# A transformer block on one core: the second feed-forward product by 15 products over thirds instead of 7 over halves, the out projection in full, the blocks in one written order

## The chip, the cores and the metric

The kernel runs on one core of one Trainium2 chip. The engines of the core that matter here: TensorE (PE) multiplies matrices, VectorE (DVE), ScalarE (ACT) and GpSimd (POOL) work element by element, and SyncE (SP) issues DMA transfers. Each engine executes its own queue of instructions in the order in which they were written; between engines they wait for each other by semaphores. SBUF is the working memory of 128 partitions, PSUM the eight banks (0 to 7) into which TensorE accumulates.

The metric is the device time of one execution, in microseconds; the numbers are medians over repeated executions.

## The reference

One block of a transformer with adaptive layer norm over 2048 tokens of 576 channels. The attention is linear (32 heads of 18 channels, a feature map from a softmax of both signs), the feed-forward part goes to 4608 channels and back:

```python
S, D, H, Dff = 2048, 576, 32, 4608
sa, ca, ga, sb, cb, gb = (silu(c) @ w_mod) in six rows of D
h = layernorm(x) * (1 + ca) + sa
q, k, v = h @ wqkv, by heads
phi(a) = concat(softmax(a @ w_phi), softmax(-(a @ w_phi)))
kv, z = phi(k)^T v, sum over tokens of phi(k)
o = (phi(q) kv) / (phi(q) z + 1e-6)
x = x + ga * (o @ wo)
h = layernorm(x) * (1 + cb) + sb
x = x + gb * (relu(h @ w1) @ w2)
```

All inputs are bf16. The two feed-forward products carry most of the work: per token 2 x 576 x 4608 multiplications.

## The kernel before

**Tiles and blocks.** The tokens are 16 tiles of 128, taken two at a time: 8 blocks of 256 tokens, numbered 0 to 7. In the first part (to about 88 us) the kernel computes the modulation, all keys and values, and `kv`; queries, softmax and the first tiles' attention follow. Then come the blocks' feed-forward parts, each a first product (`h @ w1`, relu) and a second one (`@ w2`). While block b is in its feed-forward part, the tiles of block b+1 are normalized and turned, and the attention and the out projection of block b+2 are done in between.

**Order.** All work up to the end of block 0 is written out as a list of words in a string, `ORDER`; each word stands for a function in the table `JOBS`, and the words' order is the order in which instructions are issued to the engines' queues. Blocks 1 to 7 run in a loop: `l1_seven(b, hooks)` for the first product, by another string of words (`SEVEN`), then `l2(b, hooks)` for the second. Both call hooks at numbered places, `in_seven(b)` and `in_l2(b)`, and these put the other blocks' work in.

**First product.** In blocks 1 to 7 it is computed by the seven-product scheme of Strassen and Winograd over quarters: words such as `M1_0|M5_0` are pairs of matmuls on 64 partitions (line 793), the words `A`, `B`, `C`, `d` add intermediate results on ScalarE and VectorE, and `k11_g` to `k22_g` (line 823) take the relu of a group g of four row tiles into SBUF. Four differences of the activations' quarters (`t_feat`, line 851, four instructions on VectorE) are needed ahead of it; they read `h2`, the normalized and turned tiles.

**Second product.** The relu's result of a block is a matrix of 36 row tiles (4608 channels) by 256 tokens. It is cut in halves: 18 row tiles each, 128 tokens each, and `w2` by 18 row tiles and 288 columns. The seven-product scheme needs 7 products (`prod`, line 873) of 18 matmuls of 128 x 128 weights and 288 columns: A11 B11, A12 B21, U2 T2, A11' T1, U3 T3, A22 T4 and A12' B22. The sums of weights T1 to T4 (`t_part`, line 515, 12 instructions of 1728 columns on VectorE) are made once, in block 0; the sums of activations U2 and U3 are made in each block's first product (lines 819 and 820), and A11' = A11 + U2 and A12' = A12 - U2 in its second (lines 881 and 884, 2304 columns). The products share three PSUM banks, X = 2, Y = 4 and Z = 3: bank X collects partial sums, and ScalarE copies its state out after three of the products (`copy`, line 877, tile `RS`). `fin` (lines 853 to 862) then forms an output of 128 x 288 by an addition on VectorE (line 860, or a multiplication, line 858), a multiplication with `gb` on POOL (line 861) and an addition to `x_sb` on POOL (line 862); SyncE stores the tile.

**The last block's end.** The last of the 7 products is done in two parts of 144 columns (line 910) with `gb` already multiplied into the weights (`scale_b22`), so that a single VectorE addition (line 911) and the store (line 912) follow.

**Layer norm and h turn.** In the first product of block b, the tiles of block b+1 are added up (`add_res` or `seven_add`), their mean and variance taken (`bn`, `ln2_rs`), normalized on VectorE (`ln2_apply`, line 438, two instructions per tile, tile `xn`), and turned by a DMA that SyncE issues (line 416, `h2<-xn`; in this text the h turn). In the second product of block b, ScalarE scales the nine parts of `h2` (`h_scale`, line 1045), and then `t_feat` follows.

**Attention and out projection.** In the second product of block b the attention of block b+2's tiles is finished (`num_mm`, line 404; `num_o`, lines 411 and 412) and turned by SyncE (line 416, `oT<-o_sb`). For the tiles of blocks up to 3 the out projection is `project`: 16 matmuls of 288 columns (line 957) and four on 64 partitions (line 964). In blocks 2 to 5 (`B7 = 2`) it is `seven_wo` for the blocks two further on: by the seven-product scheme, 14 matmuls (line 982) and four on 64 partitions (line 987), with sums of activations by `seven_sums` on VectorE (lines 992 to 995), copies on ScalarE (lines 1002, 1015) and additions on POOL (lines 1003, 1017). Its weight sums are `wo_sum`.

The engine queue is therefore decided by the strings and the hook positions alone; no scheduler moves anything.

## Time and profile before

| | |
|---|---|
| runs | 373.72, 372.51, 373.53 us; median 373.53 |
| profiled execution: span from its first to its last instruction | 372.0 us |
| the page names no other time of the profiled execution; median of the runs less span | 1.53 us |
| TensorE busy | 364.3 us (98%) |
| VectorE busy | 292.7 us (79%) |
| ScalarE busy | 232.9 us (63%) |
| GpSimd busy | 131.0 us (35%) |
| granted TensorE clock | full in all 40 slices |
| length of blocks 3, 4 and 5, product by product (217.77, 252.39, 287.01, 321.62 us are starts of second products) | 34.62, 34.62, 34.61 us |

The page is one profiled execution. Its busy times are means over stages with different limits, so the prediction reads windows (the busy time of each engine in a stretch of the span), the chain of work that ended last (followed back from the last instruction), groups of instructions (a line, an engine, an operation, output and inputs, shape, count, then busy time, mean duration in ns, and the idle time ahead of them with what ended it), and a few rows of the timeline (start, length, engine, line, operation, count, in brackets the wait ahead of it). PE are matmuls, PEld the weight loads that run beside them; SPq is SyncE's queue.

### The profile page before, as it was taken

How to read it: one execution, taken by the hardware profiler on the slowest of the kernel's cores; microseconds unless marked ns; L12 is line 12 of the kernel's file. 1: busy time of each engine (PE TensorE's matmuls, PEld its weight loads, DVE VectorE, ACT ScalarE, POOL GpSimd, SP SyncE). 2: the span in 40 equal slices, each digit the busy share in tenths (PEclk: the TensorE clock that was granted, in tenths of full speed). 3: DMA queues.
4: the chain of work that ended last, by engine and by line, in shares of the span. 5: the costliest groups of instructions: out<-in, count | busy, mean ns of one | idle time of the engine just before them, and what ended most of it. 6: DMA issues, size and time to landing. Idle time of an engine off the chain costs nothing.

```text
span 372.0 us, 14787 instructions
## 1 busy us (share of the span) xinstructions
PE 364.3 (98%) x6486; PEld 312.1 (84%) x6486; DVE 292.7 (79%) x538; ACT 232.9 (63%) x499; POOL 131.0 (35%) x183
## 2 busy tenths in 40 slices
...
GB/s 290 361 336 389 275 395 246 323 226 279 224 226 168 86 57 109 82 129 85 52 85 128 35 51 115 99 35 73 95 67 19 86 19 51 35 2 36 4 2 33
DMA packets 58913, 50.28 MB, mean 135 GB/s; under 512 B 46944, under 2 KB 51168, under 8 KB 58080
## 3 DMA queue, kind: packets, MB, share of 16 engines
...
q10 hardware_dynamic: 144, 0.16, 0.1%
...
HBM read 32.27 MB, written 5.90 MB: 103 GB/s over the span
## 4 chain that ended last, share of the span: by engine, by line
PE 83%; DMA 7%; DVE 5%; SPq 2%; issue 1%; ACT 1%; DVEq 0%
PE PS L873 29%; PE PS L793 27%; PE PS L282 15%; PE PS L776 4%; DMA R<-in_wqT_dram 3%; PE PS L982 2%; DMA R<-in_wsc_dram 2%; DMA oT<-o_sb 2%; SPq L363 2%; PE PS L334 2%; PE PS L404 1%; DMA eqd<-RT 1%; PE PS L957 1%; DVE R L489 1%; DVE Rq L292 1%
## 5 line engine op out<-in xcount | busy, mean ns | idle before, releaser
L861 POOL TENSOR_TENSOR yt<-yt,gb_row 128x288 f32<-128x288 f32 x23 | 27.6, 1199 | 185.8 <-DVE yt L860 185.8
L793 PEld LDWEIGHTS <-R 64*128 64x128 bf16 (+1 forms) x2128 | 88.8, 94 | 0.8 <-issue 0.2
L873 PEld LDWEIGHTS <-RH 128*128 128x128 f16 x738 | 71.1, 98 | 18.2
L793 PE MATMUL PS<-h,R 64*128 64x128 bf16 x1232 | 80.9, 216 | 0.0
L823 ACT ACTIVATE RH<-PS 128x512 f16<-128x512 f32 x112 | 59.3, 603 | 10.8 <-PE PS L793 10.7
L873 PE MATMUL PS<-R,RH 128*128 128x288 bf16 (+1 forms) x486 | 65.0, 286 | 0.0
L793 PE MATMUL PS<-RE,R 64*128 64x128 f16 x896 | 56.2, 216 | 0.0
L287 ACT ACTIVATE RT<-PS,rs 128x576 bf16<-128x576 f32 x64 | 42.5, 748 | 10.3 <-PE PS L282 9.0
L793 PE MATMUL PS<-h,early 64*128 64x128 bf16 x448 | 37.5, 216 | 0.0
L1045 ACT ACTIVATE h<-h,mod 128x256 bf16<-128x256 bf16 x63 | 32.7, 588 | 2.2 <-DMA h<-xn 2.2
L873 PE MATMUL PS<-RT,RH 128*128 128x288 f16 x252 | 33.8, 286 | 0.0
L249 DVE BATCH_NORM_STATS2 st<-x_sb 128x6 f32<-128x288 bf16 x64 | 25.7, 443 | 7.9 <-DMA x_sb<-in_xk_dram 7.8
L282 PE MATMUL PS<-RH,RT 116*128 116x288 bf16 x240 | 31.9, 286 | 0.0
L282 PE MATMUL PS<-RH,R 116*128 116x288 bf16 x240 | 31.5, 286 | 0.3
L793 PEld LDWEIGHTS <-w 64*128 64x128 f16 (+1 forms) x560 | 30.8, 94 | 0.0
L793 PE MATMUL PS<-RE,w 64*128 64x128 f16 x448 | 30.1, 216 | 0.0
L793 PE MATMUL PS<-RE,x_sb 64*128 64x128 f16 x448 | 29.2, 216 | 0.0
L793 PEld LDWEIGHTS <-early 64*128 64x128 bf16 x448 | 28.2, 94 | 0.3
L282 PEld LDWEIGHTS <-R 116*128 116x128 bf16 x240 | 22.8, 98 | 6.2 <-issue 0.3
L282 PEld LDWEIGHTS <-RT 116*128 116x128 bf16 x240 | 22.8, 98 | 5.5
L860 DVE TENSOR_TENSOR yt<-PS,RS 128x288 f32<-128x288 f32 x23 | 10.4, 450 | 20.2 <-PE PS L873 16.3
L813 ACT ACTIVATE RS<-PS 128x512 f32<-128x512 f32 x14 | 8.4, 597 | 26.8 <-PE PS L793 25.3
...
## 6 DMA issues: line engine op xcount, KB each, us to landing
...
```

The costliest lines, as they stand in the source:

```text
L249: dve.bn_stats(out=s[:, hf, :], in_=x_sb[:, t % 6 if n else t, hf * HD:(hf + 1) * HD])
L282: pe.matmul(pr[:, k, 0:HD], lhsT=xt(t, ck), rhs=w[0:R, ck, k * HD:(k + 1) * HD], start=(ck == 0), stop=(ck == NC - 1))
L287: act.activation(out=E.rearrange("p (b h s e) -> p b h s e", b=2, s=2, e=DH)[:, :, :, s, :], in_=pr[:, :, 0:HD].rearrange("p b (h e) -> p ...
L334: pe.matmul(PS[:, 6 + k, o:o + n], lhsT=E[:, c * P:(c + 1) * P], rhs=v_sb[:, t % NV, KVC[c][0] * VW:KVC[c][0] * VW + n], start=(t == 0 and ...
L776: pe.matmul(PS[:, bank_at[n], j * 256:j * 256 + 256], lhsT=w1_lhs(hi, c, j, hi), rhs=hb[64 * hi:64 * hi + 64, c, :], start=(j == 0 and c = ...
L793: pe.matmul(PS[:, bank_at[BK[n] + str(g)], i * P:(i + 1) * P], lhsT=w[r, (4 * c + i) * P:(4 * c + i + 1) * P], rhs=x, start=(n in ("M1", " ...
L813: act.activation(out=d, in_=bk["Q"], func=ACT.Copy)
L823: act.activation(out=o, in_=v[{"k11": "Y", "k12": "Z", "k21": "X", "k22": "W"}[n]], func=ACT.Relu)
L860: dve.tensor_tensor(out=y, in0=PS[:, bank, 0:HD], in1=SS[:, s, :], op=ALU.add)
L861: pool.tensor_tensor(out=y, in0=y, in1=gb_row[:, c], op=ALU.mult)
L873: pe.matmul(PS[:, bank, 0:HD], lhsT=am[:, j, :], rhs=bm[:, j, :], start=first and j == 0, stop=(j % 9 == 8), skip_group_check=True)
L1045: act.activation(out=o, in_=o, func=ACT.Identity, scale=mod(1, c), bias=mod(0, c))
```

## The change

**Thirds.** `w2` is cut in 3 x 3 blocks of 12 row tiles by 192 columns, the activations in 2 x 3 blocks of 128 tokens by 12 row tiles, and the second product is done by a scheme of 15 products of 12 matmuls of 192 columns: 180 matmuls instead of 126. 13 sums of weights (`u_sum`, 2304 columns each) are made once, in block 0, and ten sums of activations (`v_sum`) in each block; three of them are made in thirds of 512 columns, the other seven over 1536 columns. All are on VectorE. ScalarE does ten `save`s of 192 columns per block, some from PSUM to PSUM; POOL does two `merge`s; six outputs of 192 columns are finished by `fin` with 7 additions on VectorE and 12 instructions on POOL. In the last block the last product is done in two parts of 96 columns. The relu sums U2 and U3 are gone. `w2` is laid out in HBM as nine blocks and loaded in five parts.

**Out projection.** All tiles take the full one (`wo_full`, `wo_rest`); `seven_wo`, `seven_sums`, `seven_add` and `wo_sum` are gone.

**Layer norm.** The normalization of the next tiles is done on ScalarE (`ln2_bias` and `ln2_half`, two halves per tile), and the h turn is issued by SyncE in the second product. `q_sm` for tiles 6 and 7 goes from block 0 to block 1.

**Order.** Blocks 2 to 5 go by one string, `BLOCK`, for all instructions; block 1's words stand in `ORDER`, marked by `@`; blocks 6 and 7 go by `LAST`. The words of the two products' matmuls are in the same scheme as before; `P0` to `P14` are the products, `V` the sums, `S` the saves, `F` the outputs, `hs` the scaling and `tf` the feature differences. The words of `ORDER` for the attention stage change places too.

```diff
+H3 = NJ // 3
+C3 = D // 3
...
+BLOCK = """
+x0 M1_0|M5_0 M1_0|M5_0 M5_1|M5_0 M1_0|M5_0 x1 d_0 M5_1|rawhi M1_0|rawhi A_0 M5_1|M1_1 rawlo|rawhi rawlo|rawhi
...
+M4_3|M4_2 k12_1 k22_3 M3_2|r21_2 k12_3 k21_2 r21_3|r22_2 k21_3 P1 ab0 P0 S1 U_3 k22_2 U_1 P2 k12_2 P3 S2 aa0 P4 P5 nu0
+ht0 qi1 an1 ab1 S4 P6 V4 V5 V6 V7 aa1 P7 S6 no0 G V8 P8 S5 ht1 nu1 S8 F0 m1 no1 oc0 hs1 S0 m0 oT0 P9 F1 P10 hs0 S10 V9
+P11 hs5 P13 P12 hs7 oc1 V10 wf0 oT1 hs2 S13 F2 P14 hs4 hs3 tf0 S9 F4 hs6 tf1 F3 wf1 O1 hs8 tf2 F5 tf3 O0 wr
...
+    USUM = {1: (BW[1, 1], BW[0, 1], 0), 2: (BW[1, 2], US[1], 1), 3: (BW[1, 0], US[2], 0), 4: (US[3], BW[0, 1], 0),
...
+    VSUM = {1: (A10, A10, A11, 0), 2: (VA, A00, A10, 0), 3: (VB, A01, VA, 0), 4: (A01, A02, VB, 0), 5: (A10, A10, A01, 1),
+            6: (VA, VA, A11, 1), 7: (A11, A12, VA, 0), 8: (A00, A11, A00, 1), 9: (A10, A12, A01, 0), 10: (A01, A02, A11, 0)}
...
+    PROD = ((A01, BW[1, 2], "a", 1), (A00, US[6], "b", 1), (A10, US[3], "c", 1), (A02, US[8], "e", 0), (VA, US[2], "c", 0),
+            (A11, US[1], "d", 0), (VB, US[7], "f", 0), (A01, US[5], "g", 1), (VA, US[13], "c", 0), (A10, US[4], "g", 0),
+            (A11, US[10], "b", 0), (A12, US[11], "c", 0), (A10, BW[2, 1], "d", 0), (A00, US[9], "b", 0),
+            (A01, BW[2, 2], "a", 0))
+
+    def u_sum(i):
+        p, q, plus = USUM[i]
+        dve.tensor_tensor(out=US[i], in0=p, in1=q, op=ALU.add if plus else ALU.subtract)
+
+    def v_sum(i, third=None):
+        o, p, q, minus = VSUM[i]
+        if third is not None:
+            r = slice(4 * third, 4 * third + 4)
+            o, p, q = o[:, r, :], p[:, r, :], q[:, r, :]
+        dve.tensor_tensor(out=o, in0=p, in1=q, op=ALU.subtract if minus else ALU.add)
+
+    def v_third(k):
+        for i in (1, 2, 3):
+            v_sum(i, k)
+
+    def product(k, rows=range(H3)):
+        am, bm, reg, first = PROD[k]
+        for n, j in enumerate(rows):
+            pe.matmul(REG[reg], lhsT=am[:, j, :], rhs=bm[:, j, :], start=(first == 1 and n == 0), stop=(n == H3 - 1),
+                      skip_group_check=True)
+
+    def save(k):
+        reg, o, s = {0: ("a", SL[:, 0, :], 1), 1: ("b", REG["e"], -1), 2: ("c", REG["d"], 1), 4: ("c", REG["f"], -1),
...
+        act.activation(out=o, in_=REG[reg], func=ACT.Copy, scale=float(s))
...
+    def fin(i, t, eng=pool):
+        tok, n, reg, s, op = FIN[i]
+        y, c = YL[:, i % 3, :], slice(n * C3, (n + 1) * C3)
+        if op is None:
+            dve.tensor_tensor(out=y, in0=REG[reg], in1=y, op=ALU.add)
+        else:
+            dve.tensor_tensor(out=y, in0=REG[reg], in1=SL[:, s, :], op=op)
+        eng.tensor_tensor(out=y, in0=y, in1=gb_row[:, c], op=ALU.mult)
+        eng.tensor_tensor(out=xs(t + tok)[:, c], in0=y, in1=xs(t + tok)[:, c], op=ALU.add)
...
-            elif n == "U2":
-                dve.tensor_tensor(out=U3[:, j, :], in0=U3[:, j, :], in1=A11[:, j, :], op=ALU.subtract)
-                dve.tensor_tensor(out=U2[:, j, :], in0=U3[:, j, :], in1=A22[:, j, :], op=ALU.add)
+            elif n == "U":
+                v_third((0, 1, None, 2)[g])
...
-    def l2(b, hooks):
...
+    def last_half(i):
+        c = slice(i * H4, (i + 1) * H4)
+        for j in range(H3):
+            pe.matmul(PS[:, 6 + i, c], lhsT=A01[:, j, :], rhs=BH[2, 2][:, j, c], start=(j == 0), stop=(j == H3 - 1))
...
-    def seven_wo(b, k):
...
+    def ln2_half(t, d):
         o = xn[:, t % 2, :].rearrange("p (c d f) -> p c d f", d=2, f=64)
...
+        act.activation(out=o[:, :, d, :], in_=xs(t).rearrange("p (c f) -> p c f", f=64), func=ACT.Identity,
+                       scale=rs2[:, t, 0:1], bias=nrs[:, t % 2, 1:2])
...
-    for b in range(1, NB):
-        l1_seven(b, in_seven(b))
-        l2(b, in_l2(b))
...
+    for b in range(2, NB - 2):
+        do = block(b)
+        for w in BLOCK.split():
+            do(w)
```

Three places in the engines' queues. In the rows a line of the kernel, the operation, output and inputs by the program's tile names, and the shape stand; names end in a number of their buffer. The first place is ScalarE at the passage from the first to the second product of a middle block. Before: the last relus (line 823), then the copies, the scaling of `h2` (line 1045) and the small copies for the o turn (line 951).

```order
L823 ACTIVATE RH_67<-PS_104 128x4x128
L823 ACTIVATE RH_67<-PS_104 128x512 x2
L823 ACTIVATE RH_67<-PS_104 128x4x128 x3
L877 ACTIVATE RS_78<-PS_104 128x288
L1045 ACTIVATE h2_101<-h2_101,mod2_86 128x256 x3
L951 ACTIVATE o_sb_98<-o_sb_98 128x64
```

Now, in the changed kernel: the relus are line 918, the saves line 602, the halves of the normalization line 1014 (with two small ones, lines 1009 and 1010), the scaling line 1004.

```order
L602 ACTIVATE PS_103<-PS_103 128x192
L918 ACTIVATE RH_66<-PS_103 128x512 x2
L602 ACTIVATE PS_103<-PS_103 128x192
L1014 ACTIVATE xn_99<-x_sb_63,nrs_92,rs2_91 128x9x64
L1009 ACTIVATE nrs_92<-rs2_91 128x1
L1010 ACTIVATE nrs_92<-mv_88,nrs_92 128x1
L1014 ACTIVATE xn_99<-x_sb_63,nrs_92,rs2_91 128x9x64
L602 ACTIVATE PS_103<-PS_103 128x192
L1014 ACTIVATE xn_99<-x_sb_63,nrs_92,rs2_91 128x9x64
L602 ACTIVATE RS_77<-PS_103 128x192 x3
L984 ACTIVATE o_sb_97<-o_sb_97 128x64
L1004 ACTIVATE h2_100<-h2_100,mod2_85 128x256
```

The normalization stands between the relus and the scaling now; before, it stood on VectorE, ahead of these rows. The second place is VectorE in the same stretch, before:

```order
L819 TENSOR_TENSOR RH_67<-RH_67 128x512
L820 TENSOR_TENSOR RT_68<-RH_67 128x512
L881 TENSOR_TENSOR RH_67<-RT_68,RH_67 128x2304
L411 RECIPROCAL rden_97<-PS_104 128x32
L412 TENSOR_TENSOR o_sb_98<-PS_104,rden_97 128x576
```

and now (line 586 is a sum of activations, lines 612, 618 and 620 are the outputs' additions, lines 453 and 454 the attention's quotient):

```order
L586 TENSOR_TENSOR RT_67<-RH_66,RT_67 128x512
L586 TENSOR_TENSOR RH_66<-RH_66,RT_67 128x1536
L586 TENSOR_TENSOR RH_66<-RH_66 128x1536
L586 TENSOR_TENSOR RT_67<-RT_67,RH_66 128x1536
L586 TENSOR_TENSOR RH_66<-RH_66,RT_67 128x1536
L453 RECIPROCAL rden_96<-PS_103 128x32
L454 TENSOR_TENSOR o_sb_97<-PS_103,rden_96 128x576
L612 TENSOR_TENSOR yt_102<-PS_103,RS_77 128x192
```

Four sums of 1536 columns stand there in one row, ahead of the attention's quotient, where one sum of 2304 columns stood. The third place is VectorE in block 0, around its second product. Before, the attention's quotient, the last weight sums (line 515), the sum of activations (line 1129), and sums for the first product's weights (line 489):

```order
L412 TENSOR_TENSOR o_sb_98<-PS_104,rden_97 128x576
L515 TENSOR_TENSOR RT_68<-R21_66,RT_68 128x1728 x2
L1129 TENSOR_TENSOR RH_67<-RT_68,RH_67 128x2304
L489 TENSOR_TENSOR R1_64<-R1_64,w22_76 128x2048
L860 TENSOR_TENSOR yt_103<-PS_104,RS_78 128x288
```

Now, with weight sums of line 579 and sums for the first product's weights of line 531:

```order
L586 TENSOR_TENSOR RT_67<-RH_66 128x512
L579 TENSOR_TENSOR R2_65<-R2_65,RT_67 128x2304
L586 TENSOR_TENSOR RT_67<-RH_66 128x512
L586 TENSOR_TENSOR RT_67<-RH_66,RT_67 128x512
L531 TENSOR_TENSOR R1_64<-R1_64 128x2048
L586 TENSOR_TENSOR RT_67<-RH_66,RT_67 128x512 x2
L586 TENSOR_TENSOR RT_67<-RT_67,RH_66 128x1536
L586 TENSOR_TENSOR RH_66<-RH_66,RT_67 128x1536 x2
```

The last weight sums stand between the sums of activations here, and three long sums of activations stand ahead of the first output where one stood.

532 lines of the change are left out of this document (202 added, 330 removed).

## The prediction

> **What bounds the kernel now.** I read four views: the page, then the busy time by stage, then the chain that ended last, then the groups of instructions on the two engines that serve the second product. The page first.
>
> ```profile
> span 372.0 us, 14787 instructions
> PE 364.3 (98%) x6486; PEld 312.1 (84%) x6486; DVE 292.7 (79%) x538; ACT 232.9 (63%) x499; POOL 131.0 (35%) x183
> ```
>
> TensorE (PE) is busy for all but 7.7 us of 372.0. The stages tell where those are. The first three windows below are the end of the attention stage, block 0's first product and its second product; then follow three windows of one block each or nearly (blocks 3, 4 and 6; the rows give length, then busy time and instructions of each engine, clock, DMA share, GB/s).
>
> ```profile
> core 0: us, PE busy (x) PEld busy (x) DVE busy (x) ACT busy (x) POOL busy (x), PEclk, DMA share, GB/s
> 88.00:100.00 12.00, 11.51 (x202) 9.72 (x202) 11.31 (x22) 8.37 (x20) 2.27 (x2) 1.00 0.94 246
> 100.00:120.00 20.00, 19.65 (x294) 17.02 (x291) 18.61 (x32) 12.63 (x32) 0.00 (x0) 1.00 0.99 198
> 120.00:131.20 11.20, 10.86 (x91) 8.39 (x90) 11.13 (x16) 4.08 (x10) 6.36 (x7) 1.00 0.46 89
> 217.77:252.39 34.62, 34.62 (x713) 30.71 (x714) 28.24 (x56) 21.81 (x48) 11.38 (x14) 1.00 0.44 81
> 252.39:287.01 34.62, 34.62 (x713) 30.71 (x714) 28.25 (x56) 21.91 (x48) 11.38 (x14) 1.00 0.29 63
> 321.62:353.53 31.91, 31.91 (x677) 28.40 (x676) 19.65 (x32) 19.43 (x39) 7.83 (x7) 1.00 0.09 21
> ```
>
> A steady block takes 34.62 us and TensorE is busy in all of it, at full clock. There a matmul taken away is time won, as long as nothing else comes up to TensorE. Block 0 is different: from 88.00 to 131.20 VectorE (DVE) is busy 41.05 of 43.20 us, so there it runs neck and neck with TensorE. The chain gives the price of the matmuls (start, length, engine, line, count).
>
> ```profile
> 164.58 1.96 PE PS L957 x16
> ...
> 220.08 0.38 PE PS L404 x10
> ...
> 230.75 0.49 PE PS L982 x4
> ...
> 321.62 15.54 PE PS L873 x126
> ...
> 366.87 2.26 PE PS L910 x36
> 369.15 0.31 DVE x_sb L911
> ```
>
> **The products (A).** The second product is 126 matmuls of 288 columns per block, 15.54 / 126 = 123.3 ns each. The last one has 144 columns: 2.26 / 36 = 62.8 ns. A line through the two gives 62.8 + 48 x (123.3 - 62.8) / 144 = 83.0 ns for 192 columns. No 192-column matmul stands in the trace. Scaled from 288 columns alone it would be 82.2 ns; at 15.54 / 180 = 86.3 ns the 180 would cost what the 126 cost. What could stop the shorter ones is the weight load, since every matmul brings its own 128 columns of weights; but the attention's matmuls of line 404, with their own 128-column weights and at most 76 columns to stream, go at 0.38 / 10 = 38 ns. The other end is a row of the page, the weight loads of the second product by themselves, which overlap the matmuls:
>
> ```profile
> L873 PEld LDWEIGHTS <-RH 128*128 128x128 f16 x738 | 71.1, 98 | 18.2
> ```
>
> If 98 ns were what a load needs, and not what it takes while a matmul of 123 ns hides it, 180 would take 17.6 us. The attention's 38 ns lie nearer to a load that has nothing to hide behind, so I take 83.0: 180 x 83.0 = 14.94 us against 15.54, 0.60 less per block. The last block has 168 of them and 24 of 96 columns (by the same line 62.8 - 48 x 0.42 = 42.6 ns): 13.94 + 1.02 = 14.96, against 13.34 + 2.26 = 15.60, 0.64 less. Eight blocks: 7 x 0.60 + 0.64 = 4.8 us less. At 82.2 ns it is 5.9 less, and at 86.3 it is nothing.
>
> [...]
>
> **The out projection (B).** Blocks 2 to 5 have 14 matmuls of 288 columns (line 982), four of them in 0.49 us, so 1.72 us; in full it is 16 (line 957), 1.96 us. That is 0.24 more in four blocks, 1.0 us. The four short ones behind them (line 987 or 964) stay. TensorE's own sum is -4.8 + 1.0 = -3.8 us.
>
> **Block 0 (C).** The VectorE groups: mean of one is the second number behind the bar.
>
> ```profile
> L515 DVE TENSOR_TENSOR RT<-R,RT 128x1728 f16<-128x1728 bf16 x6 | 6.7, 1122 | 0.0
> L884 DVE TENSOR_TENSOR RH<-RH,RT 128x2304 f16<-128x2304 f16 x7 | 9.4, 1348 | 0.0
> L819 DVE TENSOR_TENSOR RH<-RH 128x512 f16<-128x512 f16 x28 | 11.8, 421 | 2.0 <-ACT RH L823 1.2
> L748 DVE SCALAR_TENSOR_TENSOR RH<-PS,RH 128x256 f16<-128x256 f32 x9 | 3.6, 412 | 0.4 <-ACT RH L746 0.4
> L752 DVE TENSOR_TENSOR RT<-RH 128x768 f16<-128x768 f16 x3 | 1.7, 552 | 1.0 <-DMA eqd<-RT 1.0
> L860 DVE TENSOR_TENSOR yt<-PS,RS 128x288 f32<-128x288 f32 x23 | 10.4, 450 | 20.2 <-PE PS L873 16.3 <-POOL h L1003 4.0
> L292 DVE TENSOR_REDUCE Rq<-RT 128x64 f32<-128x1152 bf16 x16 | 21.4, 1339 | 0.0
> L851 DVE TENSOR_TENSOR RE<-h 128x512 f16<-128x512 bf16 x14 | 6.7, 501 | 1.3 <-ACT h L1045 1.3
> ```
>
> Added: 13 weight sums of 2304 columns at 1.35 us (line 884 has that size) = 17.6 us; the activation sums, 9 of 512 columns at 0.42 and 7 of 1536 at 1.35 x 1536 / 2304 = 0.90, are 10.1; seven additions of 192 columns, between 0.30 (two thirds of 0.45) and 0.45, take 0.35, so 2.5. Removed: 12 weight sums of 1728 columns at 1.12 at most = 13.4; the relu sums 9 x 0.41 + 3 x 0.55 = 5.3; the two big sums 2 x 1.35 = 2.7; four of line 860, 1.8. Also two Q reductions (2 x 1.34 = 2.7) go over into block 1, as do two or three of the four feature differences (1.0 to 1.5). That is 30.2 - 23.2 - 4 = 3.0 us more in a stretch where VectorE stood only 2.15 us. Its cost is nothing if the weight sums find room before 88 us, in VectorE's gaps of the attention stage, and some 3.0 - 2.15 = 0.9, or all 3.0, if they don't. I take 1.2: the order writes most of the sums between the activation sums and not ahead of 88 us. What is late next if it falls behind is the first product that needs a late weight sum, U13 or U11, and with it TensorE.
>
> **The steady blocks (D).** The layer norm of the next tiles goes from VectorE to ScalarE (ACT), and comes later: its turning DMA, which was issued in the first product, is now issued in the second.
>
> ```profile
> L823 ACT ACTIVATE RH<-PS 128x512 f16<-128x512 f32 x112 | 59.3, 603 | 10.8 <-PE PS L793 10.7
> L877 ACT ACTIVATE RS<-PS 128x288 f32<-128x288 f32 x21 | 8.6, 410 | 21.2 <-PE PS L873 21.2
> L1054 ACT ACTIVATE xn<-x_sb,nrs,rs 128x576 bf16<-128x576 bf16 x4 | 3.3, 859 | 0.1
> L1045 ACT ACTIVATE h<-h,mod 128x256 bf16<-128x256 bf16 x63 | 32.7, 588 | 2.2 <-DMA h<-xn 2.2
> ```
>
> ScalarE gets four of line 1054's kind, 3.4 us, and ten copies of 192 columns (0.27 to 0.41, about 3.0) for three of 288 (1.2) and the out projection's three (1.2): 21.8 + 4.0 = 26 of 34 us. On the average it has room, so do VectorE (its new sums, 10.1, replace 2.7 + 4 x 0.85 of sums and four normalizations) and POOL. What counts is the queue's order at a few joins. Two rows show what VectorE and POOL do to each other:
>
> ```profile
> 223.87 1.35 DVE L884 TENSOR_TENSOR RH<-RH,RT 128x2304 f16<-128x2304 f16 x1
> 224.03 1.78 POOL L861 TENSOR_TENSOR yt<-yt,gb_row 128x288 f32<-128x288 f32 x1 [20.42 <-DVE yt L860]
> L861 POOL TENSOR_TENSOR yt<-yt,gb_row x23: 730/844/1778, 122.1 to 365.3; 128x288 f32<-128x288 f32 x23
> ```
>
> Of the group (shortest, median, longest in ns), POOL's product took 1.78 us beside a long VectorE addition, 0.73 at its shortest: it stood until VectorE was done. The new block has 14 such POOL instructions among its products (12 that finish the outputs, 2 merges) against 10 (7 of lines 861 and 862, 3 of the out projection), and seven 0.90 us additions instead of two of 1.35. [...]
>
> From the rows alone: TensorE needs the second third of the activation sums a product after the first, and the last addition to bank 3 before the next block's first matmuls of that bank. I count 0.1 to 0.3 us of wait per block for such joins, with none as the lower end since TensorE waits for none of these in the steady blocks now, and take 0.15 in five blocks: 0.75 us.
>
> **The end (E).** The last halves have 96 columns instead of 144, which saves 0.1 of the 0.31 us behind the last matmul; but six additions instead of four, on VectorE and POOL, stand just ahead of it. 0 to 0.8 us, I take 0.2, nearer the low end because line 911 starts 0.02 us after the last matmul now.
>
> **The sum.** -4.8 + 1.0 + 1.2 + 0.75 + 0.2 = -1.65 us. The span of 372.0 goes to 370.3. The median of the runs, 373.53, is 1.53 us above that span, which covers what lies around it, so I forecast 373.53 - 1.65 = **371.9 us**. Of two runs of this kernel I can't tell less than 0.3% apart, 1.1 us: faster means under 372.4, slower over 374.65.
>
> **Rivals.** First, every gain of TensorE lands: block 0's sums fit in and the joins cost nothing: 373.5 - 3.8 = 369.7 us. TensorE without a wait in all blocks now speaks for it, block 0's VectorE against it.
>
> Second, the sums and POOL eat it: block 0 costs 2.5 and the joins 0.3 in five blocks, 373.5 - 3.8 + 2.5 + 1.5 = 373.7, no change. The rows of lines 861 and 884 speak for it; against it, that the seven long additions need not all meet POOL.
>
> Third, on the other side, the h turn. Here are SyncE's issues of it (two each, 1272 ns the shortest one), ScalarE's last relus at the end of the first product, and the scaling that waits for the landing (the first row's numbers are shortest, median and longest):
>
> ```profile
> L416 SPq DMA_TRANSPOSE h<-xn x14: 1272/1292/2812, 109.5 to 321.0; - x14
> 206.88 11.51 SPq L416 DMA_TRANSPOSE h<-xn  x2
> 222.19 1.58 ACT L1045 ACTIVATE h<-h,mod 128x256 bf16<-128x256 bf16 x3 [1.67 <-DMA h<-xn]
> 241.50 11.49 SPq L416 DMA_TRANSPOSE h<-xn  x2
> 250.42 4.15 ACT L823 ACTIVATE RH<-PS 128x512 f16<-128x512 f32 x8 [0.71 <-PE PS L793]
> 255.04 1.57 ACT L1045 ACTIVATE h<-h,mod 128x256 bf16<-128x256 bf16 x3
> 276.12 11.49 SPq L416 DMA_TRANSPOSE h<-xn  x2
> 290.30 1.58 ACT L1045 ACTIVATE h<-h,mod 128x256 bf16<-128x256 bf16 x3 [0.53 <-DMA h<-xn]
> ```
>
> In block 3 the second turn is issued at 206.88 + 11.51 - 1.27 = 217.1 and has landed at 222.2, 5.1 us later; in block 5 at 286.3 and 290.3, 4.0; in block 4 at 251.7 and no later than 255.0, at most 3.3. Now the scaling waits 1.67 and 0.53 us there on ScalarE, and TensorE loses nothing. In the changed kernel the last relus end 2.2 us into the products (250.42 + 4.15 - 252.39); in the queue with them and behind them stand four halves of the normalization (0.86 each) and three saves (0.3 each), with small ones 4.6 us, so the second turn can be issued some 6.8 us in. With 3.3 us of landing the scaling begins at 10.1; its nine parts (1.57 / 3 = 0.52 each) and four saves and two small copies (1.5) take 6.2, to 16.3, and the feature differences follow. The second half lasts 14.9 + 2 x 0.38 + 1.96 = 17.6 us and four short matmuls, so all this just fits. With 5.1 all this comes 1.8 later, the saves of products 8 to 13 stand behind it in ScalarE's queue, and TensorE waits about 1.4 us per block. It decides from some 3.7 us of landing on. In blocks 1 to 5 that is 0.7 us a block at 4.0 and 1.4 at 5.1: 371.9 + 5 x 0.7 = 375.4 us, slower. For it speak the two late landings of three; against it, that at those times other DMAs (loads of x and the o turn) stood ahead, which now come elsewhere.
>
> Fourth, weight loads: at the 98 ns of line 873's loads, 373.5 + 8 x (17.6 - 15.5) + 1.0 = 391 us. Line 404 all but excludes it. [...]
>
> **Chances.** The forecast 0.36 (its own range 370.6 to 372.8), all of the gain 0.19, no change 0.18, the h turn 0.25, the weight loads 0.02. The range runs from 369.4, a little below the case of all the gain, to 375.5, a little above the h turn at 0.7 us a block; outside lie 0.08 of the former, 0.10 of the latter (landings near 5.1) and the weight loads, 0.20 in all. Faster: 0.31 of the forecast's 0.36, 0.19, and 0.02 of the no-change case, 0.52. Slower: 0.22 of the h turn's, 0.02 of the weight loads and 0.05 of the no-change case, 0.29. The rest, 0.19, is the same.
>
> **What would show it.** A matmul of 192 columns at 83 ns, 12 in 1.0 us; over 86 proves A wrong. Windows of a steady block of 34.3 to 34.5 us, with TensorE idle 0.1 to 0.3; a block over 35 with a wait of ScalarE for the h turn is the third rival. Block 0's second product late by 1 to 2 us against its block, with VectorE never idle from 88 us on, is C. Behind the last matmul 0.3 us and a store is E. The forecast is wrong if TensorE's busy time doesn't fall by about 3.8 us, or if waits of over 3 us come up in blocks 1 to 5.

## The result, and the profile after

The changed kernel takes 383.26 us (median of 4 runs, 381.32 to 386.70), the kernel before 373.31 in the same comparison (372.51 to 373.72). That is 1.028 times as long, with an interval of 1.022 to 1.033. I had forecast 371.9 us and faster: wrong in sign and by 11.4 us. The profiled execution took 386.70 us, the longest of the four (clock 0.994), with a span of 384.9; its extra over the kernel before, 12.9 us of span, is some 3 us more than the medians'. The page of the changed kernel:

```profile
span 384.9 us, 15821 instructions
PE 365.3 (95%) x6920; PEld 333.2 (87%) x6920; DVE 303.7 (79%) x533; ACT 263.6 (68%) x587; POOL 142.9 (37%) x226
```

TensorE is busy about as long as before (365.3 against 364.3), but it now stands still for 19.6 us instead of 7.7. The windows tell where (same columns as in the prediction: 3 us of the attention stage, block 0's second product, then from second product to second product of blocks 1 to 4):

```profile
89.00:92.00 3.00, 3.00 (x18) 1.96 (x16) 1.81 (x3) 2.53 (x7) 0.00 (x0) 0.64 0.44 131
117.66:137.70 20.04, 18.09 (x218) 16.82 (x220) 17.34 (x30) 10.02 (x26) 9.24 (x13) 1.00 0.44 89
154.30:189.60 35.30, 34.59 (x771) 33.41 (x769) 27.90 (x50) 25.07 (x58) 11.40 (x18) 1.00 0.47 85
189.60:226.30 36.70, 34.79 (x771) 33.41 (x768) 29.32 (x53) 25.97 (x60) 12.12 (x18) 1.00 0.44 79
226.30:263.10 36.80, 35.06 (x774) 33.46 (x769) 28.47 (x51) 26.08 (x60) 12.13 (x18) 1.00 0.43 76
263.10:298.20 35.10, 34.62 (x771) 33.47 (x768) 27.41 (x49) 25.88 (x59) 12.08 (x18) 1.00 0.33 63
```

The steady blocks are not alike any more: 36.7 and 36.8 us beside 35.1, with the same instructions. What TensorE waits for, by the view of waits (us in total, times, longest):

```profile
PE PS L888 <- issue: 3.9, 5, 1.6
PE PS L324 <- ACT RT L329: 2.0, 1, 2.0
PE PS L992 <- DMA oT<-o_sb: 1.9, 2, 1.8
...
PE PS L830 <- DVE h L698: 1.4, 1, 1.4
```

The largest has no releaser. "Issue" is time in which TensorE waited for nothing that the profile shows, in the middle of the first product's matmuls (line 888). The chain of the changed kernel shows these stops, with the products (line 595) behind them:

```profile
220.06 0.25 issue
220.31 3.75 PE PS L888 x128
224.06 1.63 issue
225.68 0.73 PE PS L888 x20
226.41 6.05 PE PS L595 x72
...
257.33 3.75 PE PS L888 x128
261.07 1.35 issue
262.43 0.73 PE PS L888 x20
263.16 6.04 PE PS L595 x72
...
269.58 2.97 PE PS L595 x36
```

Two blocks, and both times the stop stands between the same two matmuls, 20 ahead of the second product, and 128 matmuls behind the stop before it. (A third long stop, 0.48 us at 293.35 us, stands one such step earlier, 148 matmuls ahead of the next second product.) 128 matmuls with a weight load each are 256 TensorE instructions. The page counts the packets of a DMA queue that it names "instruction". Queue q8's row (packets, MB, share), first of the kernel before:

```profile
q8 instruction: 50, 0.82, 0.9%
```

and of the changed kernel:

```profile
q8 instruction: 54, 0.88, 1.0%
```

0.88 MB / 54 is 16.3 KB a packet. The changed kernel has 6920 matmuls and as many weight loads, 13,840 TensorE instructions, or 54.06 times 256; the kernel before has 12,972, 50.7 times 256. In the kernels below in which 128 matmuls are added, 256 instructions more (e9_p128 and g2_b3full), the row has 55 packets. So one packet of q8 brings 256 instructions of TensorE. I call such a packet a page of instructions, and its end the last matmul of the 128. A block of the changed kernel has 768 matmuls, 1536 instructions, exactly six pages: in every block a page ends at the same matmul. A block before has 712, 5.6 pages, so there the ends wander.

At 224.06 the page that is missing is late. The transfers that stand in its way, in the timeline of SyncE (start, length of the issue), are the ends of the q turn, an x load and the load of `eqd`:

```profile
220.22 0.33 SPq L391 DMA_DIRECT2D RT<-eqd  x1
220.65 0.39 SPq L1033 DMA_DIRECT2D x_sb<-in_xk_dram  x1
221.12 2.08 SPq L405 DMA_TRANSPOSE RE<-RT  x1
```

and the DMA view of the one microsecond from 222.9 (packets, MB, share of the 16 engines' time; over 100% means that the times of packets overlap, more of them under way than there are engines) has the page's packet among the turn's:

```profile
q1 hardware_dynamic: 480, 0.13, 306.9%
q8 instruction: 1, 0.02, 6.0%
```

The packets of q8 in this block and the two kernels to compare with, by their starts in the trace; the last column has the last three of them as time ahead of the second product (behind it where negative):

| | second product starts | packets of q8 | ahead of it |
|---|---|---|---|
| before | 217.7 | 203.0, 207.6, 211.6, 215.0, 219.6 | 6.1, 2.7, -1.9 |
| changed | 226.3 | 208.6, 213.5, 217.5, 223.5, 226.8 | 8.8, 2.9, -0.5 |
| changed, pages shifted by half (below) | 219.7 | 205.8, 210.3, 214.1, 218.7, 223.5 | 5.6, 1.0, -3.8 |

The usual distance of two packets in the first product is 3.5 to 5 us; the late one starts 6.0 after its predecessor. Against the pages: in the changed kernel's first products a packet starts 0.3 to 1.4 us behind the first matmul of a page, and brings the page behind that one; the three ahead of the long stops start 3.18, 2.81 and 1.74 us behind it. TensorE goes on 1.2 to 1.6 us after they have arrived. The two of these stops that stand in the chain cost 1.63 and 1.35 us.

All runs in one table, which the experiments refer to. The time is split where TensorE starts the second product of block 1 (P1) and of block 6 (P6): the start, five steady blocks, the end. The row of the forecast is the prediction's terms put in the same places (start: C 1.2 less 0.6 of block 0's products; blocks: five times -0.60 + 0.15, and 1.0 for B; end: -0.60, -0.64 and 0.2).

| profiled execution | start to P1 | P1 to P6 | P6 to the end | span | median of runs, ratio to before (interval) |
|---|---|---|---|---|---|
| before | 148.2 | 173.4 | 50.4 | 372.0 | 373.31 |
| forecast | 148.8 | 172.15 | 49.4 | 370.3 | 371.9 |
| changed | 154.3 | 178.9 | 51.7 | 384.9 | 383.26, 1.028 (1.022 to 1.033) |
| e4_proj | 148.3 | 174.3 | 50.5 | 373.1 | 375.00, 1.005 (1.003 to 1.007) |
| e1_loads | 150.9 | 177.7 | 52.0 | 380.6 | 382.04, 1.024 (1.020 to 1.029) |
| e3_ln | 153.1 | 174.8 | 51.9 | 379.8 | 381.27, 1.022 (1.017 to 1.027) |
| e5_noq | 153.9 | 173.7 | 51.7 | 379.3 | 380.46, 1.017 (1.014 to 1.020) |
| e2_start | 152.0 | 177.7 | 52.0 | 381.7 | 381.39, 1.022 (1.016 to 1.027) |
| e6_start | 153.1 | 177.5 | 52.1 | 382.7 | 385.52, 1.032 (1.029 to 1.036) |
| e8_phase | 151.1 | 171.7 | 51.6 | 374.4 | 376.57, 1.009 (1.006 to 1.011) |
| e9_p128 | 159.2 | 174.0 | 51.6 | 384.8 | 386.77, 1.036 (1.030 to 1.042) |
| e10_p32 | 152.2 | 172.4 | 51.5 | 376.1 | 376.83, 1.010 (1.007 to 1.012) |
| e11_p96 | 152.8 | 171.8 | 51.5 | 376.1 | 379.31, 1.016 (1.013 to 1.020) |
| s1 | 156.7 | 171.9 | 51.5 | 380.1 | 381.09, 1.022 (1.019 to 1.024) |
| c1 | 154.8 | 183.0 | 53.1 | 390.9 | 391.57, 1.047 (1.044 to 1.051) |
| g1_b3 | 152.6 | 175.8 | 51.5 | 379.9 | 381.04, 1.023 (1.020 to 1.025) |
| g2_b3full | 150.1 | 175.6 | 51.7 | 377.4 | 380.48, 1.021 (1.019 to 1.023) |
| g3_wm5 | 151.6 | 171.6 | 51.6 | 374.8 | 376.92, 1.012 (1.009 to 1.015) |

Of the changed kernel's 12.9 us, 6.1 come in the start, 5.5 in the five blocks and 1.3 at the end.

### The profile page after: what moved, and what is told of

It reads as the page before. It is cut to its first block, busy times and chain, and to the rows that moved or that the text cites. A ratio compares the mean times of both kernels' runs of the same rounds, so it can differ in the third digit from the quotient of the medians.

```text
span 384.9 us, 15821 instructions
## 1 busy us (share of the span) xinstructions
PE 365.3 (95%) x6920; PEld 333.2 (87%) x6920; DVE 303.7 (79%) x533; ACT 263.6 (68%) x587; POOL 142.9 (37%) x226
## 4 chain that ended last, share of the span: by engine, by line
PE 71%; DMA 12%; ACT 8%; issue 3%; POOL 2%; DVE 2%; SPq 1%; POOLq 0%; ACTq 0%
PE PS L888 23%; PE PS L595 19%; PE PS L324 13%; DMA h<-xn 5%; PE PS L830 5%; PE PS L871 3%; PE PS L992 3%; DMA R<-in_wqT_dram 3%; DMA eqd<-RT 2%; ACT RH L918 2%; ACT h L1004 2%; DMA R<-in_wsc_dram 2%; PE PS L376 2%; ACT xn L1014 1%; POOL yt L621 1%
## 5 line engine op out<-in xcount | busy, mean ns | idle before, releaser
L595 PEld LDWEIGHTS <-RH 128*128 128x128 f16 x1140 | 93.8, 98 | 4.3 <-issue 2.0
L888 PEld LDWEIGHTS <-R 64*128 64x128 bf16 (+1 forms) x2128 | 88.5, 94 | 6.2 <-issue 5.7
L888 PE MATMUL PS<-h,R 64*128 64x128 bf16 x1232 | 79.8, 216 | 0.0
L621 POOL TENSOR_TENSOR yt<-yt,gb_row 128x192 f32<-128x192 f32 x46 | 33.0, 718 | 91.4 <-DVE yt L618 80.9
L595 PE MATMUL PS<-R,RH 128*128 128x192 f16 (+1 forms) x660 | 62.2, 246 | 0.6 <-ACT RH L842 0.3
L586 DVE TENSOR_TENSOR RH<-RH 128x1536 f16<-128x1536 f16 (+1 forms) x56 | 42.5, 760 | 5.1 <-ACT RH L918 2.9
L595 PE MATMUL PS<-RT,RH 128*128 128x192 f16 x480 | 44.8, 246 | 1.0 <-ACT RS L602 1.0
L606 POOL TENSOR_TENSOR RS<-RS 128x192 f32<-128x192 f32 x16 | 10.1, 635 | 87.3 <-ACT RS L602 87.3
L1004 ACT ACTIVATE h<-h,mod 128x256 bf16<-128x256 bf16 x63 | 34.4, 592 | 10.7 <-DMA h<-xn 10.7
L602 ACT ACTIVATE RS<-PS 128x192 f32<-128x192 f32 x56 | 17.2, 325 | 26.1 <-PE PS L595 23.8
L622 POOL TENSOR_TENSOR x_sb<-yt,x_sb 128x192 bf16<-128x192 f32 x46 | 30.0, 653 | 3.6
```

The lines of the kernel that those rows point to most:

```text
L586: dve.tensor_tensor(out=o, in0=p, in1=q, op=ALU.subtract if minus else ALU.add)
L595: pe.matmul(REG[reg], lhsT=am[:, j, :], rhs=bm[:, j, :], start=(first == 1 and n == 0), stop=(n == H3 - 1), skip_group_check=True)
L602: act.activation(out=o, in_=REG[reg], func=ACT.Copy, scale=float(s))
L621: eng.tensor_tensor(out=y, in0=y, in1=gb_row[:, c], op=ALU.mult)
L622: eng.tensor_tensor(out=xs(t + tok)[:, c], in0=y, in1=xs(t + tok)[:, c], op=ALU.add)
L888: pe.matmul(PS[:, bank_at[BK[n] + str(g)], i * P:(i + 1) * P], lhsT=w[r, (4 * c + i) * P:(4 * c + i + 1) * P], rhs=x, start=(n in ("M1", " ...
```

## The experiments

**The out projection alone (e4_proj).** The kernel before, with the full projection in blocks 2 to 5 as well.

```diff
-    B7, WSUM = 2, {(1, 5): 0, (1, 8): 1, (1, 10): 2, (2, 1): 3}
+    B7, WSUM = 99, {}
```

> The kernel before, with the out projection of all blocks in full (16 matmuls of 288 columns instead of 14, no sums) and nothing else changed: step B of the prediction alone. The step says 0.24 us in each of four blocks, 373.3 to 374.3. Rival: the sums, copies and POOL additions that go leave room on the other engines, and the time is unchanged, 373.3; or the full projection at the block's end waits for the o turn and costs more, 376.

It took 375.00 us, 1.6 more in medians than the kernel before beside it (373.39). A window of about one of its steady blocks:

```profile
217.80:252.70 34.90, 34.90 (x722) 30.95 (x718) 26.20 (x49) 20.68 (x46) 9.31 (x11) 1.00 0.42 80
```

TensorE is busy in all of it, so the block's length is read from the starts of two second products, 218.06 and 252.92 us: 34.86 against 34.62 before, 0.24 more a block, as I had it. The spans differ by 1.1 us, where B says 1.0; the rest of the 1.6 isn't explained.

**Three edits of the steady blocks.** In e1_loads the loads of `x` and one load of `eqd` are moved to places behind the o turn and into the second product:

```diff
 BLOCK = """
-raw1 rawlo|M2_0 lx0 B_0 rawlo|M1_1 M7_0|M2_0 ...
-M5_3|M3_1 M5_3|M6_3 A_2 qi0 M5_3|M6_3 C_1 ... r21_1|M3_1 d_3 lx1 M6_2|M3_1 ...
-... k21_3 P1 ab0 P0 S1 ...
-... wf0 oT1 hs2 S13 ...
+raw1 rawlo|M2_0 B_0 rawlo|M1_1 M7_0|M2_0 ...
+M5_3|M3_1 M5_3|M6_3 A_2 M5_3|M6_3 C_1 ... r21_1|M3_1 d_3 M6_2|M3_1 ...
+... k21_3 P1 qi0 ab0 P0 S1 ...
+... wf0 oT1 lx0 lx1 hs2 S13 ...
```

> The changed kernel, with three of SyncE's issues of blocks 2 to 5 taken out of the first product: the load of the exponentials (RT<-eqd) goes ahead of product 0 and the two loads of x behind the second o turn; only the two q turns stay in the first product. Theory F (TensorE's instruction fetch is late behind these DMAs): the idle stretches that the profile ends with 'issue' in the first products of blocks 2 to 5 (0.2 + 1.9 + 1.35 + 0.5 us) shrink to under 1 us in all, and the time falls by 3 to 4 us, from 383.3 to about 379.5. Rival R (those stretches are waits for the last relus or sums that the trace doesn't show): they stay, and the time stays at 382 to 385.

The stops stayed (3.0 us in total, the longest 1.4), and the total hardly moved. A load's place in the words sets its order on SyncE's queue alone: SyncE runs ahead of TensorE, and issued `eqd` at 217.23 us, 5.8 us ahead of the second product, all the same. TensorE began a page at 217.29, and the stop of 1.35 us stands at the end of that page. So this run did not clear the place that it was meant to clear.

In e3_ln the normalization is on VectorE again, with the h turn in the first product, on top of e1_loads:

```diff
-... k12_0 k11_1 b0 M1_2|M7_1 M1_2|M7_1 M1_2|M7_1 M5_3|M7_1 k21_0
+... k12_0 l1 k11_1 b0 M1_2|M7_1 M1_2|M7_1 nd1 ht1 M1_2|M7_1 M5_3|M7_1 k21_0 l0
-... A_2 M5_3|M6_3 C_1 M2_3|M6_3 ...
+... A_2 M5_3|M6_3 C_1 nd0 ht0 M2_3|M6_3 ...
-... P1 qi0 ab0 P0 S1 ... P3 S2 aa0 P4 P5 nu0
-ht0 qi1 an1 ab1 S4 P6 V4 V5 V6 V7 aa1 P7 S6 no0 G V8 P8 S5 ht1 nu1 S8 ...
+... P1 qi0 P0 S1 ... P3 S2 P4 P5 nu0
+qi1 S4 P6 V4 V5 V6 V7 P7 S6 no0 G V8 P8 S5 nu1 S8 ...
+                "nd": lambda i: ln2_apply(n + i), ...
```

> e1_loads, and in blocks 2 to 5 the normalization of the next tiles done on VectorE in the first product again (two instructions per tile) with the h turn issued there, as the kernel before did. Theory H (the h turn issued 6.5 us into the second product lands too late for ScalarE's scaling and the saves behind it): the waits of ScalarE for h<-xn in blocks 2 to 5 (1.6 us each) go, and blocks 3 and 5 come to 34.4 us, 1 to 2 us in all below e1_loads. Rival (VectorE is full in the first product, 13.9 of 16.6 us, so 2.1 us more make its last sums late): the time is the same as e1_loads or up to 2 us more.

Now the second products of blocks 2 to 5 start 34.95 us apart, and of the stops 0.3 us is left, with the pages' ends and the q turns where they were. The five blocks take 174.8 us, 2.9 less than in e1_loads and 4.1 less than in the changed kernel. The run moved the h turn and what SyncE issues around it in one edit, so it doesn't tell what of that took the stops away. The first products behind those of blocks 2 to 4 last 17.0 us here, 16.4 in e8_phase, without a stop at the pages' ends; where that 0.6 comes from I haven't looked into.

In e5_noq the loads of `eqd` and the q turns of the steady blocks are left out (`qt0 qt1 qi0 qi1`), and with them the right queries of the later tiles.

```diff
-... B_1 qp0 qt0 k12_0 ... A_2 qi0 M5_3|M6_3 ... r12_3 qt1 M7_2|M3_3 ... ht0 qi1 an1 ...
+... B_1 qp0 k12_0 ... A_2 M5_3|M6_3 ... r12_3 M7_2|M3_3 ... ht0 an1 ...
```

> The changed kernel, with the q turns (RE<-RT) and the loads of the exponentials (RT<-eqd) of blocks 2 to 5 left out, so that in those blocks the attention works with old data; all else is issued as before. Theory F (TensorE's instructions are fetched through the same DMA engines, a page of 256 at a time, and in the first product a page lasts only 3.5 us; a burst of DMAs delays the fetch and TensorE stands): the stretches ended by 'issue' in the first products of blocks 2 to 5 go (under 0.5 us in all, 2.9 to 3.9 us in the changed kernel and e2_start), and blocks 2 to 5 take at most 139.5 us instead of 142.7 to 143.9. What then stays above 4 x 34.4 = 137.6 us is the h turn. Rival R (a wait on a semaphore that the trace doesn't show): they stay.

The stops went (0.3 us), with the pages' ends where they were. One of its blocks, and behind it what ScalarE waits for in the same kernel:

```profile
189.10:223.60 34.50, 34.50 (x770) 33.42 (x768) 28.36 (x51) 26.02 (x60) 12.12 (x18) 1.00 0.24 47
```

```profile
ACT h L1003 <- DMA h<-xn: 8.0, 7, 2.5
```

ScalarE still waits 8.0 us for the h turn (10.7 in the changed kernel), but the long waits, 2.50 and 1.96 us, stand in blocks 0 and 1. In blocks 2 to 5 it is 0.40 to 0.74 us a block, where the changed kernel has 0.62 to 1.57: with the burst, most of those waits went too. So this run ties the stops to the q turns and their loads, but it doesn't clear the h turn of the rest of the loss; that is settled below, under the rivals. What is left to test from the other side is the instruction fetch.

**Moving the pages' ends (e8, e9, e10, e11).** 64, 128, 32 or 96 matmuls of one column are added at about 17 us. They shift the ends of all later pages by a half, a whole, a quarter or three quarters of a page, and cost some 27 ns each (3.4 us for the 128 of e9_p128). Nothing else is changed.

```diff
 ORDER = """
-... FQ0:0 ...
+... ZP FQ0:0 ...
 JOBS ...
+        "ZP": lambda: spin(64, 0, 1),     (128, 32, 96)
```

> The changed kernel, with 64 matmuls of one column (128 instructions, half a page) put into TensorE's idle time at 17 us, ahead of the folding of the Q weights; nothing else. Each of blocks 2 to 4 has exactly 1536 TensorE instructions, 6 pages, so that a page ends at the same matmul in each. Theory F: the ends of pages move 64 matmuls (1.7 us) earlier in the first product, ahead of the DMA burst at its end; the stops that stood 20 matmuls before the second product in blocks 2, 3 and 4 don't stand there any more, and their sum falls from 2.9 to 3.9 us to under 1.5 us or comes elsewhere, 84 matmuls before the second product. Rival R: the stops stay where they are, 20 matmuls before the second product, with the same sum.

> As e8_phase, with 128 matmuls of one column instead of 64: 256 instructions, a whole page, so that the pages end at the same matmuls as in the changed kernel. Theory F: the stops are back, 20 matmuls before the second products of blocks 2 to 4, 2 to 4 us in all, and the time is again 381 to 387 (up to 2 us of it from the extra matmuls themselves, which don't all fit into the idle time at 17 us). Rival W (the extra matmuls help by keeping TensorE busy or its clock up early, or by shifting the early stage): it is as fast as e8_phase, 376.6, or faster.

> As e8_phase, with 32 matmuls of one column: 64 instructions, a quarter of a page, 0.9 us of the first product. Theory F: the page ends 0.9 us earlier, at the front edge of the DMA burst; the stops, if any, stand 52 matmuls before the second product and are shorter, and the time lies between e8_phase and the changed kernel, 377 to 381. Rival W: half of e8_phase's gain, 380, with the stops where they were.

> As e8_phase, with 96 matmuls of one column: 192 instructions, three quarters of a page. Theory F: the page ends 2.6 us earlier, which puts the next page's end 0.9 us after the place of the changed kernel, thus into the second product, where a page lasts 10 us and a late fetch costs nothing; the fetch before it comes ahead of the burst: 375.5 to 378, as e8_phase. Rival W: more gain than e8_phase, 374 to 375.

With half a page the kernel is 6.7 us faster in medians than the changed kernel, by work added. Two of its blocks:

```profile
151.12:185.40 34.28, 34.28 (x770) 33.39 (x768) 27.51 (x49) 24.80 (x57) 11.50 (x18) 1.00 0.40 88
219.70:254.10 34.40, 34.40 (x773) 33.52 (x770) 28.25 (x51) 26.08 (x60) 12.08 (x18) 1.00 0.35 82
```

TensorE is busy in all of both. With a quarter and three quarters the five blocks are as good (172.4 and 171.8 us against 171.7); e11_p96's total is over what was expected, and by the table that lies in the start (152.8 against 151.1). With a whole page the total went back to 386.77, as expected, but only partly for the reason expected: the blocks took 174.0, 2.3 more than with half a page but 4.9 less than in the changed kernel (its two stops are 0.26 us each), and the rest came in the start, where the 128 matmuls took 3.4 us and the clock was 0.87 in the mean from 14 to 40 us and 0.92 from 122 to 142.6. This is one of the two blocks that were slow in the changed kernel:

```profile
193.90:229.20 35.30, 34.95 (x772) 33.44 (x768) 28.48 (x52) 26.27 (x61) 12.12 (x18) 1.00 0.48 78
```

So the total of e9_p128 proves little. Since the filler stood at the very start, it could also have been the shifted times of all transfers, and not the pages, that helped. Two kernels with the filler in the middle tell these apart.

**Moving them in the middle (g1, g2).** The same 64 matmuls right ahead of block 3's first product, once in the changed kernel (from the bad place to a good one) and once in e8_phase (back to the bad one).

```diff
     for b in range(2, NB - 2):
         do = block(b)
+        if b == 3:
+            hb = h2[:, 1]
+            for _ in range(64):
+                pe.matmul(PS[:, bank_of["X0"], 0:1], lhsT=hb[:, 0, 0:P], rhs=hb[:, 0, 0:1], start=True, stop=True)
```

> The changed kernel with 64 one-column matmuls (128 TensorE instructions, half a page) right ahead of block 3's first product, their results overwritten; nothing before that point changes. Lengths from second product to second product in the changed kernel were 36.7 (block 2 to 3), 36.8 (3 to 4), 35.1, 35.0. Theory F (the place where a page of instructions ends decides): 2 to 3 takes 34.4 + 1.7 for the matmuls themselves = 36.1, 3 to 4 then 34.4, 4 to 5 and 5 to 6 34.4 each, as in the kernel with the 64 at 17 us; no stop of over 0.5 us of TensorE from block 3 on. Total some 2.5 to 4 us under the changed kernel: 379 to 381. Rival G (the kernel with the 64 at 17 us won because its transfers fell at other times from the start on): the stops stay, 3 to 4 at 36 to 37, the total 383 to 386.

> The kernel with the 64 one-column matmuls at 17 us, and 64 more right ahead of block 3's first product, so that from there on pages end again where they did in the changed kernel. Theory F: blocks up to 2 as with the 64 alone (34.3 each), 2 to 3 takes 34.4 + 1.7 + a stop, 36.3 to 37.7, and 3 to 4 34.7 to 36.5 with a stop of 0.3 to 1.6 us some 20 matmuls ahead of the second product; the total 376.6 + 1.7 + 1 to 3.5 = 379.3 to 381.8. Rival G: no stops, 3 to 4 34.4, the total 376.6 + 1.7 = 378.3 or less.

g1_b3, windows: block 2's second product with the 64 matmuls, block 3's first product, and a whole block.

```profile
189.10:209.10 20.00, 20.00 (x290) 18.92 (x288) 16.54 (x30) 12.86 (x31) 8.82 (x14) 1.00 0.36 63
209.10:225.40 16.30, 16.30 (x549) 16.10 (x548) 11.39 (x21) 12.70 (x28) 3.31 (x5) 1.00 0.38 95
225.40:259.70 34.30, 34.30 (x772) 33.47 (x768) 28.25 (x51) 25.98 (x60) 12.08 (x18) 1.00 0.37 82
```

Block 3's first product takes 16.3 us, where the changed kernel needed 18.4 (207.9 to 226.3), and the block after it 34.3 against 36.8 (the next two 34.4 and 34.3). Up to the filler this kernel has the changed kernel's instructions, and its blocks lost time (36.6 from the second product of block 1 to that of block 2, with stops of 0.46 and 0.80 us). g2_b3full goes the other way; the windows are one block ahead of the filler and two behind it:

```profile
150.10:184.60 34.50, 34.50 (x772) 33.47 (x770) 28.06 (x50) 24.89 (x58) 11.51 (x18) 1.00 0.40 88
220.80:256.00 35.20, 34.87 (x775) 33.48 (x770) 28.54 (x52) 26.24 (x61) 12.13 (x18) 1.00 0.43 80
256.00:291.30 35.30, 34.76 (x770) 33.41 (x768) 28.69 (x52) 25.95 (x60) 12.12 (x18) 1.00 0.42 66
```

34.5 became 35.2 and 35.3, with stops of 0.25 and 0.53 us. The direction is that of the pages in both runs, against the rival; the size differs, 0.8 to 1.0 us a block here and up to 2.4 in the changed kernel.

The traces of all these kernels together say what the stops are. TensorE has 35 stops of over 0.15 us named "issue" in them, and all 35 stand at the end of a page: the number of matmuls ahead of each, divided by 128, leaves 92 (91 in traces in which one matmul's record is missing), in the kernels with 32, 64, 96 and 128 more matmuls too. In e10_p32 the one stop, 0.4 us, stands 52 matmuls ahead of the second product, 32 earlier than in the changed kernel. And each of the 35 ends 1.2 to 2.0 us (33 of them 1.2 to 1.6) after a packet of q8 has arrived. The kernel before and e4_proj, whose pages' ends wander, have no such stop.

The place of the page's end decides where a stop can be. e5_noq (no burst, the bad place) and e8_phase (burst, a good place) say that it takes both; e9_p128 and e3_ln, which have both and stops of 0.3 us at most, say that both aren't enough. What differs is small. In five blocks (two of the changed kernel, two of e2_start, one of e6_start) SyncE begins to issue the second q turn 0.63 to 0.88 us behind the first matmul of a page; there the packet starts 2.15 to 3.18 us behind that matmul, and the stop is 0.8 to 1.63 us. In six others (one of the changed kernel, one of e2_start, one of e6_start, two of e9_p128, one of g2_b3full) the turn comes 0.93 to 1.07 us behind it, the packet 0.9 to 1.3, and the stop is 0.53 us at most. So a tenth of a microsecond may decide whether the packet goes ahead of the turn or behind it. That fits these blocks and was not tested; stops of 0.5 to 0.8 us also stand in three blocks in which the turn was issued ahead of the page, and the 1.35 us of e1_loads has a load of `eqd` there and no turn.

**The start (e2, e6, s1, g3, c1).** Block 0 begins late, and in more than one way. e2_start moves two weight loads (wz2, wz4) behind the stores that they were thought to delay, and wm5 behind both h turns:

```diff
-... vE14 wz2 vE15 ... us4 wr2 wz4 qp5 ... lu1 xR2 lb3 us6 ... pc1 wm5 vb4 ... pp vb5 hT2 pm0
+... vE14 vE15 ... us4 wr2 wz2 qp5 ... lu1 xR2 lb3 wz4 us6 ... pc1 vb4 ... pp vb5 hT2 wm5 pm0
```

> The changed kernel, with two loads of w2 parts issued later in the attention stage (the 1152 KB of blocks 1 and 2 from 74 us to about 92 us, the 1152 KB of blocks 7 and 8 behind it) and the last load of first-product weights (512 KB) behind both h turns of block 0 instead of between them. Theory S (w2's loads sit ahead of the exponentials' stores, whose buffers ScalarE and then TensorE wait for; the weights' load delays block 0's h turn): the eqd store lands in 3 to 4 us instead of 8, block 0's second product starts 2 to 4 us earlier than the 117.7 us of the profile, and another 1 us is won in block 0: 383.3 to about 379.5. Rival (VectorE's weight sums set that stage): the sums come later too, and the time stays at 382 to 385.

The wait for ScalarE's `RT` at 88 us was gone, but a sum then came late for the weights that were moved, and P1 was 152.0, 2.3 earlier. (In e1_loads, which leaves the start as it is, that wait was 0.2 us as well.) What TensorE waited for in block 0 of e2_start:

```profile
PE PS L595 <- DVE RH L586: 1.9, 1, 1.9
```

e6_start moves wz2 less far (ahead of `ou2`) and leaves wz4, with wm5 as in e2_start.

> The changed kernel, with one load of w2 parts (1152 KB, blocks 1 and 2) issued at about 84 us instead of 74, behind three stores of the exponentials, and the 512 KB load of first-product weights behind both h turns of block 0. Theory S: block 0's second product starts at 114 us (117.7 in the changed kernel's profile, 114.0 in that of e1_loads, where those stores happened to go ahead), and block 0's part from there to block 1 takes 18.4 us instead of 20.1, as in e2_start, without e2_start's wait for a late weight sum: 2 to 5 us in all, 379 to 380.5. Rival: what is won there is lost at the weight sums, 382.

It missed: a wait of 2.6 us for `RT` stayed, and with it came longer stretches at half clock (6.8 us in the profiled run). s1 is e8_phase with a load of first-product weights (wl3) moved behind `sq15`.

> e8_phase, with the load of 1152 KB of first-product weights that is issued at 76 us issued behind the stores of the exponentials at about 95 us. Theory S: the stores at 79 to 87 us land within 3 to 4 us instead of 6.5, ScalarE's and TensorE's waits there (1.2 us in e8_phase, with 2.0 to 2.9 us and then 3.4 or 6.8 us of half clock in the worse executions) go, and the runs come closer together: 374.5 to 375.5, all of them at full clock. Rival: the load is missed later, by a sum of weights or the first product of block 1, and the time is as e8_phase or more.

It missed as well. The load came too late: block 0's first product (line 829) waits 4.6 us for it, and the clock is at half for 3.4 us behind that. Its blocks and its end are those of e8_phase (171.9 and 51.5), so all of the loss lies in the start. g3_wm5 is e8_phase with wm5 behind both h turns, as in e2_start:

> The kernel with the 64 one-column matmuls at 17 us, and the late load of first-product weights (wm5) moved behind both h turns of block 0's second product, as in the kernel with the moved loads, where that part took 18.4 us instead of 20.1. If the h turn waits for that load there, block 1's first product starts 1 to 1.7 us earlier (132 to 132.6 instead of 133.6) and the total is 374.9 to 375.6. If block 0's wait is set by something else, 376.5 as before.

No gain (P1 151.6 against 151.1): wm5 doesn't hold block 0. c1 puts together e6_start, the normalization on VectorE in all blocks, later q sums, the loads behind the o turn, and another order of the last block's products.

> All of it together: the loads of e6_start; in blocks 1 to 6 the normalization on VectorE and the h turn early in the first product, with the mean and variance taken before the q sums; the exponentials' and x loads of blocks 2 to 5 behind the o turns; in the last block the products in an order that leaves POOL less at the end (product 10 ahead of 9, 13 ahead of 11). If the loss lies in waits (start and loads 3 to 5 us, h turn and fetch 4 to 6, the last two blocks 1 to 2), this gives 372 to 375, near the kernel before. If something else costs the time, such as VectorE's load, it stays at 379 to 382.

It is the slowest of all. VectorE is now late with what the first product waits for: by the view of waits of c1, TensorE's line 885 waits for VectorE's line 907 eight times, 3.8 us in all.

No version beat the kernel before; the best, e8_phase, is 0.9% above it.

## Why the prediction was wrong

**Bounds.** "There a matmul taken away is time won, as long as nothing else comes up to TensorE" is the sentence that failed. I checked the other engines and the transfers that instructions wait for, and not the transfer of the instructions themselves, whose row stood on the page. The count of TensorE's instructions was in the prediction as well (126 matmuls become 180), without its consequence: 112 more instructions a block, the out projection's included, and blocks of exactly six pages. The sum had no term for this. The runs show 5.1 us of it in the five blocks, by the working under D.

**A, the products: right.** The chain's rows give 72 in 6.05 us, 84.0 ns each, and 36 in 2.97, 82.5 ns; predicted 83.0. The changed kernel's page has the weight loads of line 595 at 98 ns in the mean, as line 873's were, and the matmuls follow each other at these 82.5 to 84.0 ns all the same: the fourth rival is out. (The matmuls of line 404 by which I ruled it out have 38, 76 and 95 columns and not 76 at most; their 38 ns each stand.) In the last block, from the start of the products to the last matmul, it is 15.0 us (365.7 to some 380.7), predicted 14.96. Still TensorE's busy time of the whole did not fall by 3.8 us, which I had named as the sign of a wrong forecast: it is 365.3 us, and 364.4 in e8_phase, of which some 1.7 are the filler. There the five blocks, all busy, take 1.7 us less (171.7 against 173.4; the forecast, with the joins, had 1.25 less), and the start and the last blocks take as much back; part of it is the start's half clock, the rest I haven't taken apart.

**B, the out projection: right** (0.24 a block by e4_proj, predicted 0.24).

**D, the joins: right for the steady blocks, once the stops are gone.** From the 34.62 us before, A, B and the joins gave 34.62 - 0.60 + 0.24 + 0.15 = 34.41. In e8_phase the starts of the second products of blocks 1 to 6 are 34.33 to 34.41 apart, with no idle time, so the joins cost some 0.1. Five blocks of the changed kernel take 7.2 us more than those of e8_phase (178.9 against 171.7), and the starts of the matmuls divide that in two. One page of the first product, 128 matmuls, takes 3.57 us from its first matmul to the next page's where nothing stands in the way. At seven pages' ends of the five blocks it takes 0.16 to 1.80 us longer, 5.1 us in all: the fetch. The other 2.1 lie in the second products (to the first matmul of the next block), which take 18.62, 18.18, 18.64, 17.97 and 18.55 us in blocks 1 to 5, against 17.92 to 17.97 in e8_phase: the h turn, under the rivals.

**C, block 0: the term failed in place and in size.** I expected 1.2 us from VectorE's sums, in a stretch where it would never be idle. In fact VectorE is busy 17.34 of 20.04 us in block 0's second product. To the start of that product the changed kernel is 5.05 us later than before (117.66 against 112.61), though both are level at 75.8 us. It waits 2.04 us for ScalarE's `RT` at 88 us and 1.44 for `h` at 97; between them the clock is at half for 3.4 us, 1.7 lost (the row from 89.00 has 0.64 in the mean); the kernel before lost 0.84 in two waits there. That is 4.3 of the 5.05. The first wait is for a store of `eqd`, in the chain of the changed kernel:

```profile
78.91 8.11 DMA eqd<-RT
...
93.82 1.94 ACT h L696 x4
...
96.11 1.37 DVE h L698 x4
```

8.11 us, behind two loads of 1152 KB that were issued at 74.3 and 75.4 us. e2_start, which moved the first of them, had no such wait; but neither had e1_loads, which moved none of them, so that the loads make the store late is argued and not shown. These are words of the attention stage that "change places too", and I had costed none of them, though each queue that a step is moved past should be counted. Then block 0's second product takes 1.4 us longer than before instead of 0.6. The third rival's chain sits here, as e8_phase shows it (start, length, engine):

```profile
117.95 1.63 ACT xn L1013 x2
...
121.57 4.95 DMA h<-xn
126.55 1.58 ACT h L1003 x3
...
129.61 2.56 DMA oT<-o_sb
132.22 1.16 PE PS L991 x8
```

The normalization is on ScalarE, the h turn lands late, the o turn is issued behind the scaling, and the out projection waits for it: 1.9 us in the changed kernel.

**E, the end: mis-sized.** Predicted 0.2 us, measured 1.2. Before, the last addition follows the last matmul by 0.31 us (end of matmul 369.13). Now the last matmul ends at 380.74 and POOL's last instruction at 382.25:

```profile
379.56 1.18 PE L968 MATMUL PS<-R,RH 128*128 128x96 f16 x24
380.45 0.55 POOL L961 TENSOR_TENSOR RE<-RE,x_sb 128x192 f32<-128x192 f32 x1
380.96 0.67 POOL L621 TENSOR_TENSOR yt<-yt,gb_row 128x192 f32<-128x192 f32 x1
381.70 0.55 POOL L622 TENSOR_TENSOR x_sb<-yt,x_sb 128x192 bf16<-128x192 f32 x1
```

From the last matmul's end to the last instruction ahead of the store it is now 1.5 us, 0.33 before. POOL has seven instructions in a row there, 377.58 to 382.25, and the last output stands behind all of them. I had said that six additions "stand just ahead of it" and taken the low end because VectorE had been quick; the queue that mattered was POOL's. No run changed this alone. Another part of the end's loss lies ahead of it: from block 6's second product to block 7's it takes 32.5 us, 31.9 before, where the products should have made it 0.6 shorter. Waits of 0.21 and 0.39 us stand there, which the kernel before hasn't; the rest I haven't taken apart.

**The rivals.** All the gain of TensorE (369.7) and no change (373.7) both assumed a TensorE that waits only for data. The h turn was right in its mechanism, with too high a price. It is issued 6.55 us into the products (232.96 - 226.41, predicted 6.8) and lands 4.8 us later, past the 3.7 from which I said it decides. In block 3 the chain of the changed kernel runs through it, the scaling, a save behind the scaling, POOL's merge and a sum on VectorE to TensorE:

```profile
232.96 4.84 DMA h<-xn
237.89 0.38 ACT h L1004
238.78 0.60 POOL RS L606
239.76 0.88 DVE RH L586
240.69 1.16 PE PS L595 x12
```

How much of ScalarE's wait for the turn comes up to TensorE can be read off the blocks (us; the second product as its excess over 17.97):

| | block 2 | block 3 | block 4 | block 5 |
|---|---|---|---|---|
| changed: ScalarE waits | 1.11 | 1.57 | 0.62 | 1.48 |
| second product longer by | 0.21 | 0.67 | 0.00 | 0.58 |
| e1_loads: ScalarE waits | 1.11 | 2.06 | 0.77 | 1.14 |
| second product longer by | 0.21 | 1.16 | 0.00 | 0.24 |
| e9_p128: ScalarE waits | 1.22 | 1.23 | 0.42 | 0.31 |
| second product longer by | 0.32 | 0.33 | 0.00 | 0.00 |

What the wait has over 0.90 us costs TensorE one for one, and up to there nothing. With block 1 (0.65) that is 2.1 us in the changed kernel, where the rival had 0.7 a block, 3.5. The long waits go with the place of the pages' ends as well: in blocks 2 to 5 they are 0.92 us at most in e8_phase, e10_p32 and e11_p96; in g1_b3 1.07 ahead of the filler and 0.49 behind it, in g2_b3full 0.51 ahead and 1.24 behind. By what path a stop makes the next turn land later, no run shows.

So the time came out over the range of 369.4 to 375.5 for these reasons: the stops (5.1 us), which no rival held; the h turn (2.1), which one did; a start that cost 6.1 us instead of 0.6; and the end.

**What stays open.** The start isn't settled. With the same instructions from 20 us on, P1 came at 150.9 to 154.3 us in the changed kernel, e1_loads, e8_phase, e10_p32, e11_p96 and g1_b3. Whether the waits at 88 us and the half clock start each other I can't say. Nor is it tested that a tenth of a microsecond between the page and the turn makes the difference between a stop of 1.6 us and one of 0.3.
